# Token-order phi(Q) with VectorE and GpSimd denominators and DMA transposes, for the last two chunks of a linear-attention kernel's second layer

## Chip, cores, metric

One core of one Trainium2 chip. The metric is the device time of one execution, in microseconds (us). "Span" is the time from the first to the last profiled instruction; in all runs here the time is about 1.75 us more than the span. All runs named below were at full granted TensorE clock (1.0 in the records, 0.999 in one execution of before) and of the undisturbed ("fast") state, except the single-execution run `before_again`, whose state is unknown because one execution cannot be compared with another.

## The reference, cut to what matters

Two layers, each a linear-attention block A and an MLP block B, on 2048 tokens of width 512.

```python
def _A_ref(x, wqkv, wo):                       # H = 32 heads of 16
    q, k, v = ...                              # x @ wqkv
    phi = lambda t: jnp.where(t > 0, t + 1, jnp.exp(t)) + 1e-6
    pq, pk = phi(q), phi(k)
    kv = jnp.einsum("bhsd,bhse->bhde", pk, v)
    z = jnp.einsum("bhsd->bhd", pk)
    num = jnp.einsum("bhqd,bhde->bhqe", pq, kv)
    den = jnp.einsum("bhqd,bhd->bhq", pq, z)[..., None] + 1e-6
    return merge_heads(num / den) @ wo
def _B_ref(x, w1, b1, w2, b2):                 # F = 1792, tanh gelu
    return gelu(layernorm(x) @ w1 + b1) @ w2 + b2

x = x + A(layernorm(x)); x = x + B(layernorm(x))    # layer 1
x = x + A(layernorm(x)); x = x + B(layernorm(x))    # layer 2
```

## The kernel before

The kernel is a list of named operations with dependences. A planner in its source orders them per engine by priorities (`CONF`) and by assumed durations; the engines then run in that fixed order. Tokens go in four chunks of 512, each of four tiles of 128. A name such as `pr0_1_3` is operation, layer (0 or 1), chunk, part. In the text, layer 1 is the first.

phi(Q) is made with features on the partitions ("transposed"), so that it is ready as the stationary side of the output product. Its denominators are a matmul with a masked matrix of sums, then Ln and Exp(-x) on ScalarE, then a product on VectorE:

```python
def attn_den(L, c, pq, prio):
    for kt in range(DT):
        # PE:  d = zb[kt]^T @ pq[kt]              128x128 by 128x512
        # ACT: l = Ln(d + 1e-6);  l = Exp(-l)     both 128x512
        # DVE: pq[kt] = pq[kt] * l                "pr"
        ...
```

phi itself is Exp and Relu on ScalarE, a minimum and an addition on VectorE. Each MLP tile is normalised (VectorE or ScalarE), transposed (TensorE or DMA), and GpSimd adds the second bias to the residual ahead of time; GpSimd also takes the reciprocal roots of the layer norms:

```python
    G.op("pool", lambda e: e.tensor_tensor(rstd[...], veps[...], neghalf[:], op=ALU.pow), 570, ..., name=f"pow{tag}")
    ...
    y, ykey = norm(lambda: xsb[:, st, :], ...)
    if c < cf["N_PB"]: transpose_pe(...)
    else:              transpose(...)              # DMA
    G.op("pool", lambda e: e.tensor_tensor(xsb[:, st, :], xsb[:, st, :], b2b[:], op=ALU.add), 1120, ..., name=f"b2{L}_{st}")
```

The planner stretches an operation for a busy GpSimd only if it is marked `fast`:

```python
            if o.fast and pool_busy > at:
                dur += min(pool_busy - at, 600.0)
```

TensorE is started with eleven dummy matmuls (`warm`).

## Time and profile before

| | before |
|---|---|
| median of 3, at first | 338.05 us (337.94 to 339.32) |
| span of the profiled execution | 337.5 us (its time was 339.3) |
| TensorE, VectorE, ScalarE, GpSimd busy | 98, 58, 76, 31% |

From the profile page of the kernel before, the busy times and the chain of work that ended last:

```profile
PE 329.7 (98%) x1810; PEld 162.9 (48%) x1810; DVE 196.7 (58%) x431; ACT 255.0 (76%) x413; POOL 103.7 (31%) x197
...
PE 82%; DVE 9%; ACT 3%; POOL 3%; DMA 1%; issue 1%; DVEq 0%
```

PE is TensorE, PEld its weight loads, DVE VectorE, ACT ScalarE, POOL GpSimd. TensorE bounds the kernel. But "busy" overlaps neighbouring matmuls (the page gives one a mean of 379 ns, from start to start it is 216), so it does not show the small holes. Starts do. The TensorE timeline of the kernel before (start, duration, engine, line, operation, shapes, count):

```profile
303.08 12.25 PE L778 MATMUL ps<-t,w 128*128 128x512 bf16 x56
315.16 16.78 PE L816 MATMUL ps<-w,gT 128*128 128x512 bf16 x77
331.78 3.22 PE L803 MATMUL ps<-w,gT 128*128 128x256 bf16 x28
```

77 matmuls from 315.16 to 331.78 are 0.216 us each; the 256, 128 and 1-column ones are 0.109, 0.056 and 0.025 us. I price every matmul so. What is left between two starts is called a **hole**. The sum of the prices is TensorE's work, the sum of the holes is what waiting costs. (Some profiles lack 32 of TensorE's matmul records, one in about every 10.8 us; the weight-load records are complete and tell where; a missing matmul is put in at its price.)

The groups of instructions that the change touches (line, engine, operation, tiles, shapes, count, then busy us and mean ns, then idle time before):

```profile
L735 DVE TENSOR_TENSOR t<-t,lr 128x512 bf16<-128x512 bf16 x32 | 21.9, 684 | 14.9 <-ACT lr L733 14.8
L731 ACT ACTIVATE lr<-ps,eps 128x512 f32<-128x512 f32 x32 | 21.9, 685 | 4.7 <-PE ps L729 4.5
L764 POOL TENSOR_TENSOR xsb<-xsb,b2b 128x512 f32<-128x512 f32 x32 | 37.9, 1191 | 10.4 <-ACT yb L533 6.2
```

A last reading, from the chain of waits (start, duration, what). TensorE waits for a DMA transpose that took 3.97 us, where the median is 2.5:

```profile
150.02 1.25 DVE yb L538
...
151.30 3.97 DMA t<-yb
155.27 0.05 issue
155.32 2.76 PE ps L778 x12
```

### The profile page before, as it was taken

The numbers are of one execution on the slowest core, as the hardware profiler recorded it, in microseconds if no ns is written. First come the engines' busy times: TensorE is split into PE (matmuls) and PEld (weight loads), VectorE is DVE, ScalarE is ACT, GpSimd is POOL, SyncE is SP. The second block draws the span as 40 slices with busy tenths as digits, with TensorE's granted clock in tenths as the row PEclk, the third lists the DMA queues.
The fourth block names the chain that finished last, engine by engine and source line by source line (L and its number), as shares of the span: only waits on it lengthen the run. The fifth ranks groups of instructions, "written<-read, shape, count | busy, mean of one in ns | idle before, by whom it ended". The sixth has DMA issues, their size and how long they took to land.

```text
span 337.5 us, 4893 instructions
## 1 busy us (share of the span) xinstructions
PE 329.7 (98%) x1810; PEld 162.9 (48%) x1810; DVE 196.7 (58%) x431; ACT 255.0 (76%) x413; POOL 103.7 (31%) x197
## 2 busy tenths in 40 slices
PE   7899999999999999998999999999999999999997
PEld 3444443566544444443444445458644444444444
DVE  6899568969175383583516679996072481820112
ACT  2988699989999979943995299979997689547300
POOL 5743400786125041183102200078400450360000
PEclk9999999999999999999999999999999999999999
DMA  8722660011110021032100110000210120130011
GB/s 269 244 52 60 234 218 0 3 40 26 31 32 18 15 47 17 0 62 57 23 16 5 29 31 2 1 2 16 49 47 16 21 60 17 33 62 16 15 50 47
DMA packets 32996, 16.71 MB, mean 50 GB/s; under 512 B 26636, under 2 KB 32012, under 8 KB 32972
## 3 DMA queue, kind: packets, MB, share of 16 engines
q1 hardware_dynamic: 29404, 9.19, 11.9%
q0 software_dynamic: 1056, 4.72, 4.0%
q10 hardware_dynamic: 2512, 2.49, 2.3%
q8 instruction: 14, 0.23, 0.3%
q14 instruction: 10, 0.08, 0.1%
HBM read 8.00 MB, written 2.10 MB: 30 GB/s over the span
## 4 chain that ended last, share of the span: by engine, by line
PE 82%; DVE 9%; ACT 3%; POOL 3%; DMA 1%; issue 1%; DVEq 0%
PE ps L778 27%; PE ps L816 24%; PE ps L600 7%; PE ps L616 5%; PE ps L748 5%; PE ps L681 4%; PE ps L650 4%; DVE yb L538 2%; DVE stats L514 2%; DVE xsb L753 2%; PE ps L729 2%; PE ps L505 1%; ACT eb L582 1%; DMA t<-yb 1%; DVE t L735 1%; POOL xsb L764 1%
## 5 line engine op out<-in xcount | busy, mean ns | idle before, releaser
L778 PE MATMUL ps<-t,w 128*128 128x512 bf16 (+1 forms) x560 | 101.8, 336 | 1.2 <-DMA t<-yb 0.9
L816 PE MATMUL ps<-w,gT 128*128 128x512 bf16 x434 | 98.9, 379 | 0.0
L784 ACT ACTIVATE gT<-ps,b1c 128x512 bf16<-128x512 f32 (+1 forms) x140 | 78.3, 602 | 16.4 <-PE ps L778 15.7
L778 PEld LDWEIGHTS ps<-t,w 128*128 128x128 bf16 x560 | 54.3, 98 | 45.4 <-DMA t<-yb 1.6
L816 PEld LDWEIGHTS ps<-w,gT 128*128 128x128 bf16 x434 | 42.3, 98 | 49.9 <-DVE xsb L822 0.2
L582 ACT ACTIVATE eb<-ps 128x512 bf16<-128x512 f32 x64 | 38.6, 616 | 17.7 <-PE ps L600 14.6
L948 ACT ACT_TABLE_LOAD x33 | 42.3, 1283 | 0.6
L764 POOL TENSOR_TENSOR xsb<-xsb,b2b 128x512 f32<-128x512 f32 x32 | 37.9, 1191 | 10.4 <-ACT yb L533 6.2
L584 ACT ACTIVATE rb<-ps 128x512 bf16<-128x512 f32 x64 | 39.0, 620 | 1.9 <-PE ps L616 1.9
L526 POOL TENSOR_TENSOR rstd<-veps,neghalf 128x1 f32<-128x1 f32 x64 | 37.1, 580 | 7.3 <-DVE veps L524 2.4
L519 POOL TENSOR_SCALAR veps<-mv 128x1 f32<-128x1 f32 x32 | 6.9, 214 | 97.9 <-DVE mv L516 96.6
L586 DVE TENSOR_SCALAR eb<-eb 128x512 bf16<-128x512 bf16 x64 | 19.1, 305 | 28.6 <-ACT eb L582 28.1
L514 DVE BATCH_NORM_STATS2 stats<-xsb 128x6 f32<-128x512 f32 x48 | 32.8, 684 | 1.0
L600 PE MATMUL ps<-wqkv,t 128*128 128x512 bf16 x128 | 32.7, 379 | 0.5 <-ACT t L571 0.4
L616 PE MATMUL ps<-t,wqkv 128*128 128x512 bf16 x128 | 32.0, 379 | 0.2 <-ACT t L571 0.2
L748 PE MATMUL ps<-gtb,t 128*128 128x512 bf16 x128 | 31.3, 379 | 0.5 <-DVE gtb L665 0.5
L735 DVE TENSOR_TENSOR t<-t,lr 128x512 bf16<-128x512 bf16 x32 | 21.9, 684 | 14.9 <-ACT lr L733 14.8
L524 POOL TENSOR_SCALAR veps<-mv 128x1 f32<-128x1 f32 x29 | 7.4, 255 | 73.9 <-DVE mv L516 73.6
L538 DVE TENSOR_SCALAR yb<-xsb,mv,rstd 128x512 bf16<-128x512 f32 x24 | 17.8, 744 | 18.4 <-POOL rstd L526 18.0
L826 DVE TENSOR_TENSOR outb<-ps,xsb 128x512 bf16<-128x512 f32 x15 | 10.3, 690 | 30.7 <-PE ps L816 30.6
L533 ACT ACTIVATE yb<-xsb,nmr,rstd 128x512 bf16<-128x512 f32 x24 | 19.3, 812 | 11.6 <-POOL nmr L530 9.1
L731 ACT ACTIVATE lr<-ps,eps 128x512 f32<-128x512 f32 x32 | 21.9, 685 | 4.7 <-PE ps L729 4.5
(61 smaller groups left out, 297.1 us busy)
## 6 DMA issues: line engine op xcount, KB each, us to landing
w<-in_B_w_dram POOLq DMA_DIRECT2D x4, 896.0 KB, 8.8
out_dram<-outb SPq DMA_DIRECT2D x15, 128.0 KB, 1.7
t<-in_A_x_dram ACTq DMA_DIRECT2D x3, 512.0 KB, 7.9
t<-yb SPq DMA_TRANSPOSE x48, 2.5
wqkv<-in_A_wqkv_dram SPq DMA_DIRECT2D x1, 512.0 KB, 5.2
wqkv<-in_A_wqkv_dram ACTq DMA_DIRECT2D x1, 512.0 KB, 6.9
wqkv<-in_A_wqkv_dram POOLq DMA_DIRECT2D x1, 512.0 KB, 5.9
wo<-in_A_wo_dram POOLq DMA_DIRECT2D x1, 512.0 KB, 5.4
```

The source lines that it names most:

```text
L514: G.op("dve", lambda e: e.bn_stats(stats[:, s.slot, :], src()), 620, reads=src_keys, writes=[k + "s"], tiles=[s, *src_tiles], prio=prio, n ...
L526: G.op("pool", lambda e: e.tensor_tensor(rstd[:, s.slot:s.slot + 1], veps[:, s.slot:s.slot + 1], neghalf[:], op=ALU.pow), 570, reads=[k + ...
L582: G.op("act", lambda e: e.activation(eb[:, et.slot, :], bank(bt), ACT.Exp), 478, reads=[src_key], writes=[f"e{tag}"], tiles=[bt, et], prio ...
L584: G.op("act", lambda e: e.activation(rb[:, rt.slot, :], bank(bt), ACT.Relu), 478, reads=[src_key], writes=[f"r{tag}"], tiles=[bt, rt], pri ...
L600: ins = e.matmul(bank(b), lhsT=yTa(yT)[:, dt, k * P:(k + 1) * P], rhs=wqkv[:, dt, D:2 * D], start=(dt == 0), stop=(dt == DT - 1))
L616: ins = e.matmul(bank(b), lhsT=wqkv[:, dt, kt * P:(kt + 1) * P], rhs=yTa(yT)[:, dt, :], start=(dt == 0), stop=(dt == DT - 1))
L748: ins = e.matmul(bank(wb), lhsT=yTa(pq)[:, kt, k * P:(k + 1) * P], rhs=gtb[:, kt, :], start=(kt == 0), stop=(kt == DT - 1))
L764: G.op("pool", lambda e: e.tensor_tensor(xsb[:, st, :], xsb[:, st, :], b2b[:], op=ALU.add), 1120, reads=[("x", st), "b2b"], writes=[("x", ...
L778: ins = e.matmul(bank(b, n), lhsT=w1[:, dt, ft * P:(ft + 1) * P], rhs=yTa(yT)[:, dt, k0 * P:k1 * P], start=(dt == 0), stop=(dt == DT - 1))
L784: G.op("act", lambda e, ft=ft, b=b, k0=k0, k1=k1, n=n: e.activation(gT[:, g.slot, ft * 512 + k0 * P:ft * 512 + k1 * P], bank(b, n), ACT.Ge ...
L816: ins = e.matmul(bank(b), lhsT=gT[:, g.slot, ft * 512 + k * P:ft * 512 + (k + 1) * P], rhs=w2[:, ft, :], start=(ft == 0), stop=(ft == FT - 1))
L948: e.preload_act_table_set(sets[table])
```

## The change

The intent is to take denominator work from TensorE and ScalarE. For chunks 2 and 3 of layer 2, Q is computed with tokens on the partitions. The denominators are then sums along the free axis: a product with a row of sums that one matmul broadcasts to all partitions, a reduction per head, an addition, a reciprocal, a scaling; a DMA transpose brings the result to the layout that the output product needs. The same diff adds a table (`WAY`) of which engine does what, moves phi additions, products, normalisations and copies between engines in both layers, gives three MLP transposes to the DMA, and re-tunes every priority.

```diff
-    N_HALF=1, N_K=1, N_Q=2, P_Z0=0, N_PB=1, N_PT=8, P_DEN=-58.92, P_A2=-10.01, ...
+    N_HALF=1, N_K=1, N_Q=2, P_Z0=0, N_PB=1, N_PT=8, P_DEN=-55.81, P_A2=-10.5, ...
     SHIFT={ ... every entry re-tuned ... },
+    WAY={ "TB1_0": "pe", "TB1_1": "dma", "TB1_2": "dma", "TB1_3": "dma", ...
+        "den1_2": "tok", "den1_3": "tok", ...
+        "phiq0_0_3": "pool", "phiq0_1_2": "pool", "phiq0_2_0": "pool", ...
+        "pr0_0_2": "pool", "pr0_1_0": "pool", "pr0_2_2": "pool", ...
+        "pz1_2_1": "pool", "pr1_2_2": "pool", ... },
@@ attn_q
+            if by_token(L, c):
+                for k in range(4):   # lhsT = tokens of tile k, rhs = all 512 columns of wq
+                    ...
@@ attn_kv
+                # DVE: dz = identity * sums;  PE: ones^T @ dz;  ACT: zrow = copy
@@ attn_den
+            if by_token(L, c):
+                for k in range(4):
+                    # pz : lr = pq * zrow                 GpSimd or VectorE
+                    # red: rd = sum of lr per head        VectorE
+                    # den: rd += 1e-6; rec: rr = 1 / rd   VectorE
+                    # pr : pq *= rr (per head)            GpSimd or VectorE
+                    # TP : DMA transpose into a new tile
```

## The prediction

> **What bounds it now.** TensorE: the page gives it 98% of the 337.5 us span, at full granted clock. "Busy" flatters (a matmul's modelled 379 ns overlaps the next), so I used start-to-start times in the TensorE timeline: seven 512-column matmuls take 1.51 us, 0.216 each. [...] Pricing every matmul so, real work is about 321.4 us. The other 16: 6.4 until the warm-up ends, about 7 of holes, 2.8 after the last matmul starts. Of the holes, 2.7 lie before 20 us, 2.3 at 49 to 81 (layer-1 attention to MLP), 1.1 at 154 (a wait for a DMA transpose), 0.9 at 210 to 225 (layer change). From 226 us to the end, where chunks 2 and 3 of layer 2 are normalised, TensorE has no hole.
>
> **Removed.** Eight denominator matmuls (1.73 us of TensorE); eight Ln (685 ns) and eight Exp (631 ns) on ScalarE, 10.5 us; eight 684 ns VectorE products. ScalarE loads tables nine times (1283 ns each) after 225 us, six of them from 270 to 286, where chunk 3's denominators alternate with Gelu; I expect four fewer. None of this is on the path: TensorE waits for nothing there.
>
> **Moved.** Q for these chunks has the same 32 matmuls. Three of layer 2's four MLP transposes of chunk 0 go from TensorE (0.23 us each) to DMA: 0.69 us less. Products, phi additions and normalisations move between VectorE, ScalarE and GpSimd; priorities are re-tuned.
>
> **Added.** One broadcast matmul (0.22), one ScalarE copy (0.60), one VectorE product (0.69). Per token tile: product, reduction, two small operations, scaling, DMA transpose. Estimates from like operations in the trace: 0.68 for each large one on VectorE, or 1.2 on GpSimd (1191 ns measured), 0.15 to 0.2 for the small ones, 2.5 for a transpose; about 6 us latency per tile. VectorE gains some 10 us and gives most of it back to GpSimd, whose load rises from 104 to about 140. The output products of chunks 2 and 3 start at 259 and 287, their Q is done by 221 and 275: the latency can be hidden. [...]
>
> **On the path.** Only TensorE's work and holes count: -1.73 + 0.22 - 0.69 = -2.2 us. Re-tuning should shave holes by perhaps 0.5 to 1 us, most likely at the layer changes. Sum: 338.05 - 2.9 = 335.2 us.
>
> **Prediction: 335.2 us, range 333.0 to 338.0.** Faster by over 2%: 0.05; within 2%: 0.92; slower by over 2%: 0.03.
>
> **What would show it.** Denominator matmuls 32 to 24; TensorE work priced as above 319.2; ScalarE busy down 12 to 17 us, table loads 33 to about 28; GpSimd up about 35; 59 DMA transposes instead of 48; no TensorE hole between 230 and 330; the chain of waits over 80% TensorE. The gain should equal the lost matmuls plus the change in holes, not the ScalarE saving.
>
> **What would make it wrong.** New holes: GpSimd's longer queue delays the layer norms' reciprocal roots, so MLP transposes come late; a token tile's chain queues behind other DMA work and the output product waits; VectorE, 95% busy at 200 to 230, lengthens the layer change. Or the holes at 50 to 81 and 154 close wholly: up to 3 us more.

-1.73 + 0.22 - 0.69 is -2.2 us of work, about -0.7 of holes makes -2.9, and 338.05 - 2.9 gives the 335.2. The prices are those of the starts in the trace (0.216, 0.109, 0.056 and 0.025 us, see above).

## The result, and the profile after

| | before | after |
|---|---|---|
| median of 6 | 338.0 us | 339.27 us |
| range | 337.87 to 339.32 | 338.6 to 339.58 |
| ratio | | 1.0028, 95% interval 1.0011 to 1.0046 |

A ratio is the mean time of one kernel's runs over that of the other's of the same rounds, so it is not quite the ratio of the medians. The kernel became 0.3% slower, clear of noise in these rounds, where 0.8% faster was forecast. The size is less sure than the sign: before's times fall in two groups (see the experiments), and only one of the six here is of the upper one. Against all 39 executions of before (mean 338.70 us), the mean of the changed kernel, 339.20, is 0.15% longer. What it failed to be is faster.

The profile page of the changed kernel:

```profile
PE 325.9 (96%) x1759; PEld 161.4 (48%) x1791; DVE 201.9 (60%) x433; ACT 242.7 (72%) x392; POOL 141.1 (42%) x228
...
PE 75%; DVE 10%; POOL 8%; ACT 3%; issue 2%; DMA 1%; POOLq 0%
```

The intended shift took place: ScalarE lost 12 us, GpSimd gained 37, VectorE 5. But the share of the chain held by TensorE fell from 82 to 75%, and GpSimd's rose from 3 to 8%. The new token operations, from the groups of the changed kernel:

```profile
L821 DVE TENSOR_REDUCE rd<-lr 128x32 f32<-128x512 f32 x8 | 5.3, 672 | 3.7 <-POOL lr L819 3.7
...
L819 DVE TENSOR_TENSOR lr<-t,zrow 128x512 f32<-128x512 bf16 x5 | 4.3, 877 | 0.0
...
L819 POOL TENSOR_TENSOR lr<-t,zrow 128x512 f32<-128x512 bf16 x3 | 3.5, 1153 | 0.1
```

The reductions and GpSimd's products cost what was estimated. The mean of VectorE's products, 877 ns, holds one that was stretched to 1.64 us; the other four took 0.68 to 0.69, as estimated. The reciprocals took 0.34 us, where 0.15 to 0.2 was estimated. And, in the last column, VectorE's reductions waited 3.7 us for GpSimd's products.

The kernel before was profiled a second time later (`before_again`), on a usual execution; it is the fairer partner. TensorE's account, in us:

| holes between | before, first profile | before, second profile | after |
|---|---|---|---|
| 0 and 48 us | 5.13 | 5.16 | 5.17 |
| 48 and 58 | 1.46 | 1.46 | 2.06 |
| 58 and 70 | 0.43 | 0.42 | 0.93 |
| 70 and 90 | 0.43 | 0.43 | 1.07 |
| 90 and 150 | 0.10 | 0.10 | 0.00 |
| 150 and 165 | 1.11 | 0.00 | 1.02 |
| 200 and 230 | 0.88 | 0.88 | 0.57 |
| 240 and 260 | 0.00 | 0.00 | 1.22 |
| all holes | 9.53 | 8.45 | 12.04 |
| priced work from 6.4 us on | 321.26 | 321.20 | 319.08 |
| span | 337.50 | 336.42 | 337.85 |

TensorE's work fell by 2.12 us, as predicted. Its holes grew by 3.59 us. The difference, 1.47 us, is the growth of the span (1.43) to the rounding. So the question is where four groups of holes come from: 48 to 58, 58 to 90, about 155, and 240 to 260 us.

The same from the view of stretches (window, its length, busy us of each engine with counts, clock, DMA share, GB/s), the second profile of the kernel before:

```profile
48.00:90.00 42.00, 40.70 (x261) 23.67 (x263) 31.47 (x61) 40.07 (x74) 19.39 (x33) 1.00 0.10 20
150.00:165.00 15.00, 14.95 (x70) 6.77 (x70) 7.52 (x15) 7.77 (x10) 5.88 (x12) 1.00 0.27 54
240.00:260.00 20.00, 19.95 (x94) 9.06 (x93) 8.52 (x16) 17.50 (x27) 2.27 (x2) 1.00 0.14 39
```

and the changed kernel:

```profile
48.00:90.00 42.00, 38.80 (x253) 22.83 (x255) 31.17 (x55) 38.84 (x73) 25.40 (x39) 1.00 0.08 17
150.00:165.00 15.00, 14.10 (x66) 6.27 (x65) 9.35 (x16) 6.46 (x9) 7.50 (x15) 1.00 0.30 45
240.00:260.00 20.00, 19.02 (x90) 8.64 (x91) 17.06 (x33) 15.00 (x21) 11.40 (x13) 1.00 0.40 93
```

The first column after the length is TensorE. In the last stretch GpSimd went from 2.3 to 11.4 us busy and VectorE from 8.5 to 17.1.

**Around 53 us**, in layer 1, which the token path does not touch. GpSimd, VectorE and TensorE of the changed kernel:

```profile
52.59 1.15 POOL L643 TENSOR_TENSOR t<-eb,rb 128x512 bf16<-128x512 bf16 x1
```

```profile
53.01 1.28 DVE L850 TENSOR_TENSOR t<-t,lr 128x512 bf16<-128x512 bf16 x1 [0.57 <-ACT lr L846]
54.22 1.27 DVE L737 TENSOR_SCALAR gtb<-ps 128x512 bf16<-128x512 f32 x2
```

```profile
54.95 1.42 PE L865 MATMUL ps<-gtb,t 128*128 128x512 bf16 x5 [1.42 <-DVE gtb L737]
```

In the kernel before, the same product takes 0.69 us:

```profile
52.97 0.69 DVE L735 TENSOR_TENSOR t<-t,lr 128x512 bf16<-128x512 bf16 x1
```

In the changed kernel GpSimd adds a phi that VectorE used to add (0.41 us there). VectorE's product, 0.68 us when alone, starts at 53.01 and ends at 54.29: 0.55 us after GpSimd's operation has ended at 53.74. The copy `gtb` that TensorE waits for comes after it. I call such an operation **stretched**. Over the whole span, 12 VectorE operations before were over 0.15 us longer than the fast tenth of their own group, 9.2 us in sum, and 26 after, 17.8 us. All 26 start while a GpSimd operation runs, and they end 0.04 to 0.55 us after its end: the products 0.55 us, the phi additions 0.28. (11 of the 26 have two tensor inputs; the other 15, normalisations for the most part, have one.) That the GpSimd operation beside them is the cause is tested below (`l1_back`, `tiny_bias`); by what mechanism it stretches them no trace here shows.

**Around 247 us**, where chunk 3's token work runs. VectorE of the changed kernel:

```profile
241.12 0.69 DVE L821 TENSOR_REDUCE rd<-lr 128x32 f32<-128x512 f32 x1 [1.72 <-POOL lr L819]
241.72 1.41 DVE L643 TENSOR_TENSOR t<-eb,rb 128x512 bf16<-128x512 bf16 x1
...
244.69 0.59 DVE L824 TENSOR_SCALAR rd<-rd 128x32 f32<-128x32 f32 x1
...
245.71 1.20 DVE L830 TENSOR_TENSOR t<-t,rr 128x512 bf16<-128x512 bf16 x1
246.83 1.27 DVE L943 TENSOR_TENSOR outb<-ps,xsb 128x512 bf16<-128x512 f32 x2
248.03 1.16 DVE L639 TENSOR_SCALAR eb<-eb 128x512 bf16<-128x512 bf16 x1
```

GpSimd beside it:

```profile
239.93 1.15 POOL L819 TENSOR_TENSOR lr<-t,zrow 128x512 f32<-128x512 bf16 x1
241.69 1.15 POOL L881 TENSOR_TENSOR xsb<-xsb,b2b 128x512 f32<-128x512 f32 x1 [0.61 <-ACT yb L577]
244.20 1.05 POOL L830 TENSOR_TENSOR t<-t,rr 128x512 bf16<-128x512 bf16 x1 [1.35 <-DVE rr L826]
245.21 3.83 POOL L881 TENSOR_TENSOR xsb<-xsb,b2b 128x512 f32<-128x512 f32 x3
```

and TensorE:

```profile
247.57 1.04 PE L865 MATMUL ps<-gtb,t 128*128 128x512 bf16 x4 [0.68 <-DVE outb L943]
...
250.30 1.04 PE L933 MATMUL ps<-w,gT 128*128 128x512 bf16 x4 [0.19 <-DVE xsb L870]
```

VectorE loses 1.7 us waiting, in order, for a GpSimd product, and 2.9 us to four stretched operations (three beside a bias addition, L881, one beside a token scaling, L830). So it comes late to `outb`, which frees the PSUM bank (one part of `ps`, where TensorE's results land) that TensorE needs: TensorE waits 0.68 us for it.

**Around 155 us.** The chain of waits of the changed kernel shows the slow DMA transpose of before's first profile again:

```profile
152.84 4.02 DMA t<-yb
156.86 0.05 issue
156.91 1.25 PE ps L895 x5
```

### The profile page after: what moved, and what is told of

The parts are those of the page before. It is cut to its first block, busy times and chain, and to the rows that moved or that the text cites. A ratio compares the mean times of both kernels' runs of the same rounds, so it can differ in the third digit from the quotient of the medians. Undisturbed runs are those within 1.5% of the kernel's fastest.

```text
span 337.9 us, 4861 instructions
## 1 busy us (share of the span) xinstructions
PE 325.9 (96%) x1759; PEld 161.4 (48%) x1791; DVE 201.9 (60%) x433; ACT 242.7 (72%) x392; POOL 141.1 (42%) x228
## 3 DMA queue, kind: packets, MB, share of 16 engines
q1 hardware_dynamic: 35388, 10.63, 14.4%
## 4 chain that ended last, share of the span: by engine, by line
PE 75%; DVE 10%; POOL 8%; ACT 3%; issue 2%; DMA 1%; POOLq 0%
PE ps L895 23%; PE ps L933 21%; PE ps L656 7%; PE ps L865 5%; PE ps L687 4%; PE ps L753 4%; PE ps L721 4%; DVE xsb L870 3%; POOL rstd L569 2%; POOL xsb L881 2%; DVE stats L557 2%; PE ps L674 2%; PE ps L541 1%; DVE yb L582 1%; POOL nmr L574 1%
## 5 line engine op out<-in xcount | busy, mean ns | idle before, releaser
L895 PE MATMUL ps<-t,w 128*128 128x512 bf16 (+1 forms) x552 | 100.2, 336 | 2.2 <-DVE xsb L939 0.9
L933 PE MATMUL ps<-w,gT 128*128 128x512 bf16 x424 | 97.3, 379 | 0.7 <-DVE xsb L870 0.2
L901 ACT ACTIVATE gT<-ps,b1c 128x512 bf16<-128x512 f32 (+1 forms) x140 | 79.5, 602 | 20.1 <-PE ps L895 19.8
L569 POOL TENSOR_TENSOR rstd<-veps,neghalf 128x1 f32<-128x1 f32 x64 | 38.1, 595 | 7.5 <-DVE veps L567 2.5
L881 POOL TENSOR_TENSOR xsb<-xsb,b2b 128x512 f32<-128x512 f32 x32 | 37.9, 1188 | 6.4 <-DVE yb L582 4.4
L1065 ACT ACT_TABLE_LOAD x31 | 39.8, 1283 | 0.5
L637 ACT ACTIVATE rb<-ps 128x512 bf16<-128x512 f32 x63 | 38.3, 618 | 0.0
L639 DVE TENSOR_SCALAR eb<-eb 128x512 bf16<-128x512 bf16 x63 | 20.0, 327 | 22.5 <-ACT eb L626 22.1
L582 DVE TENSOR_SCALAR yb<-xsb,mv,rstd 128x512 bf16<-128x512 f32 x24 | 19.1, 797 | 15.5 <-POOL rstd L569 15.3
L687 PE MATMUL ps<-t,wqkv 128*128 128x512 bf16 x95 | 23.6, 379 | 0.3 <-ACT t L615 0.2
L870 DVE TENSOR_TENSOR xsb<-ps,xsb 128x512 f32<-128x512 f32 x16 | 10.7, 677 | 16.1 <-PE ps L865 15.8
L865 PEld LDWEIGHTS ps<-gtb,t 128*128 128x128 bf16 x128 | 12.2, 98 | 17.0 <-DVE gtb L737 3.0
```

The lines of the kernel that those rows point to most:

```text
L569: G.op("pool", lambda e: e.tensor_tensor(rstd[:, s.slot:s.slot + 1], veps[:, s.slot:s.slot + 1], neghalf[:], op=ALU.pow), 570, reads=[k + ...
L637: G.op("act", lambda e: e.activation(rb[:, rt.slot, :], bank(bt), ACT.Relu), 478, reads=[src_key], writes=[f"r{tag}"], tiles=[bt, rt], pri ...
L687: ins = e.matmul(bank(b), lhsT=wqkv[:, dt, kt * P:(kt + 1) * P], rhs=yTa(yT)[:, dt, :], start=(dt == 0), stop=(dt == DT - 1))
L865: ins = e.matmul(bank(wb), lhsT=yTa(pq)[:, kt, k * P:(k + 1) * P], rhs=gtb[:, kt, :], start=(kt == 0), stop=(kt == DT - 1))
L895: ins = e.matmul(bank(b, n), lhsT=w1[:, dt, ft * P:(ft + 1) * P], rhs=yTa(yT)[:, dt, k0 * P:k1 * P], start=(dt == 0), stop=(dt == DT - 1))
L901: G.op("act", lambda e, ft=ft, b=b, k0=k0, k1=k1, n=n: e.activation(gT[:, g.slot, ft * 512 + k0 * P:ft * 512 + k1 * P], bank(b, n), ACT.Ge ...
```

## The experiments

Theories: (A) the engine moves of layer 1 make holes, because VectorE operations that start beside a GpSimd operation are stretched (0.68 to 1.28 us at 53 us); (B) the re-tuned order makes them; (C) the token work of chunk 3 makes the hole at 247 us; (D) the hole at 155 us belongs to the DMA. With before's table put into the changed source, all five engines have exactly before's order of operations, so the parts of the change could be undone one by one. In most edits below TensorE's order stays, or changes in two places. Ratios are to the runs of before in the same rounds; before's medians there were 338.39, 338.89 and 338.48 us. Its runs fall in two groups, 337.8 to 338.9 and over 339.1 us (14 of 39 executions). Before's mean moved from 338.24 to 338.89 us from one set of rounds to another, so differences of under 0.5 us between medians of different sets mean little. The holes are each of one profiled execution.

| run | time, us | ratio (95%) | all holes | 48-58 | 58-90 | 150-165 | 240-260 |
|---|---|---|---|---|---|---|---|
| after | 339.27 | 1.0028 (1.0011, 1.0046) | 12.04 | 2.06 | 2.00 | 1.02 | 1.22 |
| l1_back | 338.29 | 0.9985 (0.9962, 1.0008) | 10.67 | 1.46 | 1.79 | 0.80 | 1.15 |
| tok3_late | 337.95 | 0.9979 (0.9955, 1.0003) | 11.25 | 2.06 | 2.01 | 1.29 | 0.14 |
| both | 337.27 | 0.9958 (0.9935, 0.9981) | 9.69 | 1.46 | 1.80 | 0.78 | 0.14 |
| dummies | 341.68 | 1.0085 (1.0060, 1.0111) | 12.76 | 2.05 | 2.01 | 1.28 | 1.07 |
| before_again | 338.16 | one execution | 8.45 | 1.46 | 0.85 | 0.00 | 0.00 |
| tiny_bias | 337.73 | 0.9965 (0.9940, 0.9990) | 10.25 | 2.06 | 2.00 | 0.46 | 0.00 |
| both_ord (= both) | 337.22 | 0.9947 (0.9924, 0.9970) | 9.94 | 1.46 | 1.78 | 0.85 | 0.15 |
| tok_dve | 337.95 | 0.9974 (0.9949, 0.9999) | 10.40 | 2.05 | 2.00 | 0.92 | 0.00 |
| order_back | 336.45 | 0.9933 (0.9915, 0.9951) | 8.92 | 1.46 | 0.60 | 1.04 | 0.14 |
| fetch_both | 336.68 | 0.9942 (0.9924, 0.9960) | 9.16 | 1.46 | 1.81 | 0.00 | 0.29 |
| fetch_before | 338.25 | 0.9989 (0.9971, 1.0006) | 8.71 | 1.46 | 1.36 | 0.00 | 0.00 |
| best | 335.67 | 0.9919 (0.9900, 0.9938) | 8.14 | 1.46 | 1.12 | 0.00 | 0.00 |

### l1_back

```diff
-        "phiq0_0_3": "pool", "phiq0_1_2": "pool", "phiq0_2_0": "pool", ... "pr0_3_3": "pool",
+        "phiq0_0_3": "dve", "phiq0_1_2": "dve", "phiq0_2_0": "dve", ... "pr0_3_3": "dve",   # 11 entries
```

> Eleven operations of layer 1 that the change gave to GpSimd (six additions of phi(Q), five products with the reciprocal) go back to VectorE; the order of TensorE's work stays. [...] TensorE holes between 48 and 90 us fall from 4.1 to about 2.6 us, the stretched VectorE operations at 53.0, 80.5 and 84 us go back to 0.7 us, time 1 to 1.5 us below the changed kernel, about 338.0. Rival (the re-tuned order alone made the holes, the engine does not matter): holes stay at 4 us, time stays at 339.3. Second rival (VectorE is short of time there): holes grow, time 340 or more.

(What stood to the test is theory A as given above.)

The time fell by 1.0 us. VectorE around 53 us, in this run:

```profile
52.36 0.41 DVE L643 TENSOR_TENSOR t<-eb,rb 128x512 bf16<-128x512 bf16 x1
52.73 0.69 DVE L850 TENSOR_TENSOR t<-t,lr 128x512 bf16<-128x512 bf16 x1
53.34 1.28 DVE L737 TENSOR_SCALAR gtb<-ps 128x512 bf16<-128x512 f32 x2
```

The addition is done on VectorE and the product is whole again at 0.69 us, although VectorE has one operation more there; the hole at 53 us is exactly before's 1.46. So the engine, not the order, made that part. (The planner could not see it: as the code above shows, it does not stretch a product `pr` for a busy GpSimd.) But between 58 and 90 us only 0.2 us came back, not the 0.9 expected: theory A explains 0.8 us of layer 1's 1.75.

### tok3_late and both

```diff
-        "D13": -12.6,
+        "D13": 47.4,
```

> The changed kernel with the priority of chunk 3's token work lowered by 60, so that VectorE and GpSimd do it after 250 us rather than between 240 and 250; order of TensorE's work unchanged. Theory (that work crowds out the two VectorE operations that free and feed TensorE at 247 and 250 us): holes between 240 and 260 us fall from 1.2 to under 0.3 us and no new hole appears before the output product of chunk 3, time about 338.3. Rival (GpSimd's bias additions make the hole whatever VectorE does there): hole stays near 1.2 us. Rival (the token chain was needed that early): a new hole of 1 us or more before 300 us.

The hole fell from 1.22 to 0.14 us, no other appeared, and the time fell by 1.3 us. The work was not needed so early. (The hole at 155 us was 0.27 us longer.)

`both` has the edits of `l1_back` and `tok3_late`.

> Both edits together. If the two causes are separate, the savings add: TensorE holes from 12.0 to about 9.5 us as before the change, time 336.8 to 337.2, which is the before time less the 2.2 us of TensorE work that the change removes, plus what the profile of the changed kernel already shows beyond the span (its time is 1.4 us over its span against 0.5 before in most runs). If they overlap: 338.

337.27 us: 2.0 us below the changed kernel, where the sum of the two would be 2.3. It beats the kernel before, but by 0.4%. TensorE's holes are still 1.2 us above those of before's second profile. My estimate in that expectation of how time and span differ (1.4 and 0.5 us) rested on mixing a profiled time with other runs' medians; the difference is about 1.75 us for both kernels.

### dummies

```diff
+                    bd = Tile(psum, f"d{tag}", "n")
+                    G.op("pe", lambda e, tok=tok, bd=bd: e.matmul(bank(bd), lhsT=zb[:, 0:P], rhs=tok(), start=True, stop=True), ...)
```

> The changed kernel plus eight unused 512-column matmuls, one for each token tile, in place of the eight denominator matmuls that the change removed. If TensorE work is worth its full price: plus 1.7 us, about 341.0, holes unchanged. If TensorE has slack around chunks 2 and 3 that would hide them: under 0.5 us.

The time grew by 2.4 us: 1.73 of priced work (eight matmuls of 0.216 us) and 0.7 of holes. The holes are not unchanged as expected: a dummy reads a finished token tile, and one at 284 us waited 0.95 us for it, a wait that the edit brought in. The point holds: removed TensorE work is worth its full price here, so the token path did earn its 1.5 us, and lost it elsewhere.

### before_again

> The kernel before, unchanged, for a second profile: its first one fell on a run of 339.3 us where most take 337.9 to 338.4. If the slow profile hides 1.3 us somewhere, a profile of a usual run shows 1.3 us fewer TensorE holes than 9.5 (about 8.2), and the place where they went is where runs of one kernel differ (start-up loads or the wait for a DMA transpose at 154 us). If it lands on a slow run again, 9.5.

This execution took 338.16 us with a span of 336.4, and has 1.08 us less of holes than the first profile, nearly all of it at 154 us. From 141 to 154 us the timelines of the engines differ by about 0.03 us; only the transpose issued at 151.3 us differs: 3.97 us against 2.45.

### tiny_bias

Its output is wrong, which doesn't matter for the time.

```diff
-            G.op("pool", lambda e: e.tensor_tensor(xsb[:, st, :], xsb[:, st, :], b2b[:], op=ALU.add), 1120,
+            G.op("pool", lambda e, n=(1 if L == 1 and st < 8 else D): e.tensor_tensor(xsb[:, st, 0:n], xsb[:, st, 0:n], b2b[:, 0:n], op=ALU.add), 1120,
```

> The changed kernel with every operation in its place, but GpSimd's bias additions of layer 2 for the first eight token tiles work on one column in place of 512 (the result is wrong on purpose). These are the GpSimd operations beside which four VectorE operations between 240 and 250 us were stretched by 0.5 to 1.0 us. [...] the stretches go away (2.9 us of them fall to under 0.6) and the TensorE holes at 247 and 250 us fall from 1.2 to under 0.3 us; time about 338.2. Rival (VectorE has simply too many token operations there): stretches gone or not, the hole stays above 0.8 us.

(The cut word named theory A.)

The stretches between 240 and 260 us fell from 2.9 to 0.5 us and the hole vanished, with all of VectorE's token work still in place. The span lost 1.8 us: 1.2 are this hole and 0.6 a shorter transpose wait at 155 us.

### tok_dve

```diff
-        "pz1_2_1": "pool", "pz1_3_2": "pool", "pr1_2_2": "pool", "pr1_2_3": "pool", "pr1_3_2": "pool",
+        "pz1_2_1": "dve", "pz1_3_0": "dve", "pz1_3_2": "dve", "pr1_2_2": "dve", "pr1_2_3": "dve", "pr1_3_2": "dve",
```

(An entry that is absent for `pz` means GpSimd, so six operations moved; the expectation says five.)

> The changed kernel with the five token products that GpSimd does given to VectorE. If GpSimd's token work makes the hole at 247 us: it falls under 0.4 us. If VectorE is crowded there and the bias additions hold it up: two more VectorE operations of 0.7 us before 247 us, so the holes between 240 and 260 us grow from 1.2 to 1.9 to 2.6 us and the time to about 340.3.

My own forecast was wrong and the rival right: with more work on VectorE the hole vanished. VectorE in this run:

```profile
241.30 1.68 DVE L830 TENSOR_TENSOR t<-t,rr 128x512 bf16<-128x512 bf16 x1
...
243.28 1.27 DVE L830 TENSOR_TENSOR t<-t,rr 128x512 bf16<-128x512 bf16 x1
244.55 0.69 DVE L943 TENSOR_TENSOR outb<-ps,xsb 128x512 bf16<-128x512 f32 x1
```

Bias additions still stretch VectorE (1.7 us of it), but it no longer waits in order for a GpSimd product, and comes to `outb` at 244.55 instead of 246.83 us. Three single edits each remove this hole: fewer bias stretches, no hand-overs to GpSimd, or the work later. The hole is the end of a sum of delays, each of them larger than the 0.85 us piece at 247 us. No single one is "the" cause.

### both_ord and order_back

The run `both_ord` was meant to have three operations moved. By a slip the kernel was `both` itself, so it only repeats it (337.22 against 337.27 us).

> The kernel with both edits, and three operations of layer 1 put back in the places that they had before the change: a product with the reciprocal on VectorE after the statistics of the next tile, another such product after the statistics of layer 2's first tile, and one bias addition on GpSimd behind the reciprocal root of the next tile. Theory (the re-tuned order of VectorE and GpSimd made the rest of the layer-1 holes): holes between 58 and 90 us fall from 1.8 to about 0.9 us, time from 337.3 to about 336.4. Rival (they come from somewhere else): no change.

`order_back` is the kernel that was meant:

```diff
         order = sch.run()
+        for en, a, b in [('dve', 'pr0_1_3', 'aggrB0_1'), ('dve', 'pr0_2_1', 'statsA1_0'), ('pool', 'b20_2', 'powB0_7')]:
+            names = [o.name for o in order[en]]
+            o = order[en].pop(names.index(a))
+            names.remove(a)
+            order[en].insert(names.index(b) + 1, o)
```

> What the run named both_ord was meant to be (that one was, by a slip, the kernel with both edits once more): both edits, and three operations of layer 1 back in their places of before. Theory (the re-tuned order of VectorE and GpSimd makes the rest of the layer-1 holes): holes between 58 and 90 us fall from 1.8 to about 0.9 us, time from 337.25 to about 336.4. Rival (they come from elsewhere): no change.

Holes between 58 and 90 us fell from 1.80 to 0.60 us, below before's 0.85, and the time to 336.45 us. About 0.7 us of that is the hole at 81 us. The edit moved two VectorE products and one bias addition at once; for this hole the traces point to the bias addition (L881). It stood ahead of a reciprocal root on GpSimd, and VectorE's normalisation `yb` waited for that root. GpSimd and VectorE in `both`:

```profile
73.60 2.50 POOL L881 TENSOR_TENSOR xsb<-xsb,b2b 128x512 f32<-128x512 f32 x2
77.04 1.37 DVE L582 TENSOR_SCALAR yb<-xsb,mv,rstd 128x512 bf16<-128x512 f32 x1 [1.95 <-POOL rstd L569]
```

and in `order_back`:

```profile
73.27 1.20 POOL L881 TENSOR_TENSOR xsb<-xsb,b2b 128x512 f32<-128x512 f32 x1
75.47 1.37 DVE L582 TENSOR_SCALAR yb<-xsb,mv,rstd 128x512 bf16<-128x512 f32 x1 [0.72 <-POOL rstd L569]
```

So theory B holds for this hole, and `best`, with the same order, has it closed too. The other 0.5 us, at 62 us, is not shown to be the order's: it is back in `best`, and `fetch_before` has it with before's own order (see there).

### fetch_both and fetch_before

The DMA records of the traces show a second user of the DMA engines: a queue of kind "instruction" with 14 packets of 16 KB (a second such queue has packets of 8 KB). On the changed kernel's page:

```profile
q8 instruction: 14, 0.23, 0.2%
```

The changed kernel has 1791 weight loads and as many matmuls on TensorE, 3582 instructions, which over 14 packets is 256 for each; and between two of the packets 116 to 140 weight loads with their matmuls start, on average 257 instructions in 23.2 us. So I take these packets for TensorE's own instructions; that is an inference from the counts. From the same counts, 26 instructions more should move a packet by about 2.3 us, an estimate; the expectation for `fetch_both` says 2.5. Worked out from the records (not a view of the profile):

| run | transpose issued, us | took, us | nearest 16 KB fetch, us | hole, us |
|---|---|---|---|---|
| before, first | 151.30 | 3.97 | 153.1 | 1.11 |
| before_again | 151.33 | 2.45 | 153.5 | 0.00 |
| after | 152.84 | 4.02 | 154.5 | 1.02 |
| both | 151.79 | 3.79 | 152.9 | 0.78 |
| order_back | 150.77 | 4.05 | 151.9 | 1.04 |
| fetch_both | 151.58 | 2.41 | 147.9 | 0.00 |
| fetch_before | 151.34 | 2.42 | 148.4 | 0.00 |
| best | 150.85 | 2.42 | 147.2 | 0.00 |

In before, whose fetch comes 1.8 or 2.2 us after the issue, 0.4 us decides. Over all 14 traces, 21 of the 25 transposes with such a fetch between 1.0 and 2.4 us after their issue took 2.9 us or more; of the 768 others, 62. With the 8 KB packets counted too, every one of these 83 slow transposes has an instruction packet that starts between its issue and its landing (to 0.02 us), and 57 of the 710 quicker ones have.

```diff
-            for _ in range(11):
-                ins = e.matmul(bank(wu), lhsT=onesm[:, 0:P], rhs=onesm[:, :], start=True, stop=True)
+            for n in [D] * 9 + [1] * 15:
+                ins = e.matmul(bank(wu, n), lhsT=onesm[:, 0:P], rhs=onesm[:, 0:n], start=True, stop=True)
```

> The kernel with both edits, with the eleven warm-up matmuls replaced by nine and fifteen one-column ones: 26 TensorE instructions more, so that every 16 KB instruction fetch falls some 2.5 us earlier against the work. Theory (the fetch at 153 us is what makes the DMA transpose issued at 152 us take 3.8 us in place of 2.4, and TensorE waits for it): fetch at about 150.3 us, that transpose under 3 us, hole at 154 us falls from 0.8 to under 0.3 us, time about 336.6. Rival (the transpose is slow there for another reason): hole stays at 0.8 us.

> The same exchange of warm-up matmuls in the kernel before. Its times fall in two groups, about 338.0 and 339.2 to 340.3. If the upper group is the fetch at 153.1 us falling into the last transpose that TensorE waits for: all runs in the lower group, no hole at 154 us, spread under 0.7 us. If the groups have another cause: both groups again.

Both holes at 155 us went to zero. The fetches moved by 5 us, twice what was expected; why is open. New holes came elsewhere: 0.2 to 0.3 us between 165 and 187 us in `fetch_both`, `fetch_before` and `best`, and in `fetch_before` 0.5 us at 62 us, where a reciprocal root on GpSimd took 1.12 us in place of 0.55. `fetch_both` gained 0.6 us on `both`. `fetch_before` stayed in the lower group in all six executions (337.84 to 338.74 us); with 14 of 39 in the upper group, six in the lower by chance would be about 7%, so the trace, not the count, carries this. The slow transpose is shown to go with the fetch; that all executions of before in the upper group are this collision is likely, with one profile of each group, not shown.

### best

The edits of `l1_back` and `tok_dve`, the three moved operations of `order_back` and the warm-up of `fetch_both` in one; `tok3_late`'s is left out.

> All that helped, in one: the eleven layer-1 operations and the five token products back on VectorE, the three operations of layer 1 in their old places, and the earlier fetch. If the causes are separate: TensorE holes about 7.9 us, span 333.7, time 335.5. If the exchange of warm-up matmuls costs clock or start-up time: 336.5 or more.

335.67 us, ratio 0.9919 to before (about 0.993 to the runs of before's lower group alone): 3.6 us below the changed kernel. The granted clock was 1.0 in all six executions, with the new warm-up too. Its page and its stretches:

```profile
PE 326.8 (98%) x1804; PEld 161.4 (48%) x1804; DVE 207.2 (62%) x450; ACT 242.1 (73%) x392; POOL 124.3 (37%) x211
...
PE 84%; DVE 5%; POOL 5%; ACT 4%; issue 1%; DMA 1%; POOLq 0%
```

```profile
48.00:90.00 42.00, 40.65 (x263) 23.56 (x262) 32.29 (x60) 39.78 (x74) 19.94 (x33) 1.00 0.10 20
150.00:165.00 15.00, 15.00 (x71) 6.84 (x70) 8.70 (x17) 8.05 (x10) 5.78 (x11) 1.00 0.25 50
240.00:260.00 20.00, 20.00 (x97) 9.22 (x95) 13.46 (x28) 15.34 (x21) 9.32 (x11) 1.00 0.40 92
```

TensorE holds 84% of the chain again, and is busy all through the last two stretches. The sum of VectorE's stretching does not tell the time: it was 9.2 us before, 17.8 after, and is still 14.4 here, in the fastest run, where VectorE's share of the chain that ended last is 5%, not 10. One thing did not carry over: the hole at 62 us is 0.88 us here and 0.38 in `order_back`. A one-column reciprocal root on GpSimd took 1.12 us in place of 0.55; in `best` a VectorE product started 0.03 us after it, in `order_back` too. The same happens with before's order: 0.55 us in its two profiles, 1.12 in `fetch_before`. What decides between the two the profile does not show. It is left open.

## Why the prediction was wrong, point by point

- **Wrong: the term for the holes.** The step was: "Re-tuning should shave holes by perhaps 0.5 to 1 us". The holes grew by 3.59 us against a usual execution of before. Its pieces: 0.60 at 48 to 58 us (GpSimd's phi addition, shown by `l1_back`); 0.64 at 70 to 90 (about 0.2 the engines, shown by `l1_back`, the rest the order, shown by `order_back` and `best`); 0.50 at 58 to 70 (one stretched reciprocal root, which before's own order shows as well in `fetch_before`: the cause stays open); 1.02 at 155 (instruction fetch beside a DMA transpose, shown by `fetch_both`; the first profile of before has it too, and so have all nine profiles of the changed kernel and its variants with the old warm-up, 0.46 to 1.29 us. No term of the prediction was about where the fetch falls: this piece is bad luck); 1.22 at 240 to 260 (chunk 3's token work at a bad moment, shown by `tok3_late`, `tiny_bias` and `tok_dve`); less 0.31 at 200 to 230 and 0.10 at 90 to 150.
- **Wrong: "no TensorE hole between 230 and 330"** and "the chain of waits over 80% TensorE" (75%). I argued that the token chain's latency can be hidden, which is true, and forgot that its operations share in-order queues with the VectorE operations that free PSUM banks (at 241 us VectorE waited 1.72 us for a GpSimd product, at 247 us TensorE 0.68 us for `outb`). Latency was hidden; the occupancy was not.
- **Right: what bounds the kernel, and the size of the work removed.** 319.08 us measured, 319.2 predicted; 24 denominator matmuls; 59 DMA transposes. ScalarE's 12.3 us appear nowhere in the account of work and holes, which closes without them. `dummies` shows that TensorE's work counts fully.
- **Right in kind:** of the three dangers named for new holes, the first came true (late reciprocal roots of the layer norms, at 81 us); VectorE operations stretched beside GpSimd did too (9.2 us before, 17.8 after). The other two, the transpose that waits behind DMA work and a longer layer change, did not. I gave them no weight in the sum, and a range that reached 2.8 us above the forecast; the result was 4.1 us above it.
- **Wrong, without effect:** table loads (1283 ns each) fell from 33 to 31, not to about 28. GpSimd gained 37 us (35 predicted).
- **A slip of reading:** the profile of before was of a 339.3 us execution while the median was 338.05. I counted its 1.1 us hole at 154 us as always there.

The change's core, token order for two chunks, was not at fault as such: with the same TensorE work, `best` takes 335.67 us. That this is near the 335.2 forecast does not bear the forecast out: `best` has other engines and another order than the predicted kernel, and the moved fetch, worth 0.6 us in `fetch_both`, is no part of undoing the change.

## What to carry to other kernels

When one engine is 98% busy, count its work and its holes apart: here the work removed paid in full (2.12 us less of it; eight matmuls put back cost their 1.73), but the engine moves, the re-ordering and a fetch at a bad moment opened 3.59 us of holes that the busy percentage did not show. The GpSimd operations given "for free" were paid for by VectorE operations that started beside them (0.68 us became 1.28 at 53 us), and by the in-order hand-over (1.72 us at 241 us); check both for what lies on the bounding engine's chain. Profile both groups of a kernel whose times fall in two groups before you subtract one profile from another.
